# Attention with SyncE in written order: the queries' transposing DMA goes to the head of the next pair, and whole-batch loads are spread differently over two pairs

## The chip, the core and the metric

One core of a Trainium2 chip runs the whole program. Engines are named as in the profile: PE (TensorE), DVE (VectorE), ACT (ScalarE), POOL (GpSimd) and SP (SyncE, which issues nearly all DMAs here). The metric is device time in microseconds (us) of one execution.

## The reference

Three stages follow each other: block-causal attention, a soft mixture of experts, and a feed-forward layer with a squared ReLU. Inputs and outputs are float32; the change touches the first stage alone.

```
q, k, v: (8, 8, 576, 64)
scores = q @ k.T / sqrt(64)
scores = where(block_i >= block_j, scores, -1e9)
scores = scores - max(scores, -1)
attn = exp(scores)
x = attn / (sum(attn, -1) + 1e-9) @ v
x = x.transpose(0, 2, 1, 3).reshape(4608, 512)
x = soft_moe(x, phi, w1, w2)
out = square(relu(x @ w_in)) @ w_out
```

Blocks are 64 positions long, so a row sees whole blocks up to its own.

## The kernel before

Attention works on two heads at a time: 32 pairs, four for each of the 8 batches. In the code `n` is the pair, `bn` its batch and `jn` its place in the batch (0 to 3). `pair(n)` (L997) writes out the steps of one pair in eight slots, and several pairs are under way at once: in `pair(n)` stand the score matmuls of pair n (`scores`, L546), the products with V of pair n-1 (`pv`, L610), the row maxima of pair n+2 (`maxpass`, L468) and the splitting of pair n+3 into fp16 parts (`split`, L419).

A score is the sum of two fp16 matmuls. The first uses the high parts, `t1` and `s1`. The second uses `t2` and `s2`: `t2` holds the low part of the queries and two columns with the negated row maximum, `s2` the keys with constant rows. Both of these come by DMA. The rows are written into `qb` (three buffers), and one DMA transposes `qb` into `t2` (two buffers, by the parity of the pair). `s2copy(n)` (L956) copies the upper half of `s1` into `s2` (two buffers). The keys' own transposing DMA into `s1` stands in `prep_k` (L451) and is issued in slot 0 of the pair three ahead of its own.

The last step of a maximum is `fin` (L521), in slot 6: DVE reduces the partial maxima, writes two columns of `qb` (L531, L534), and the transposing DMA into `t2` follows at once, at L539. It waits for L534 and, since `t2` is reused, for the second matmuls of the pair two before.

Before any of that, `scale` (L373) takes the sums of squares of q and k: ACT squares (L379, written to `junk`), one PE matmul (`ps_ssq`, L386) and eight small DVE steps (L391 to L408) give the factors that `split` needs. In a pair with odd n this is done for two pairs, four and five ahead.

PE and SP run in the order in which the program writes their instructions; DVE, ACT and POOL are ordered by the scheduler. SP's order is set by `pair(n)`: `s2copy(n + 1)` first, then the eight slots. Loads wait as functions in the list `dq`, and `loads(k)` takes the next k of them: three in slot 0 before the slot's steps, one after each of slots 1 to 5, two after slots 6 and 7. Into `dq` go the V loads of pair n+2 (`load_v`, two, or four in the first pair of a batch), the loads of the batch after next (`load_batch`, L351: for k and for q two tails and four main parts of 256 KB each), all of k in the second pair of a batch and all of q in the third, and from pair 7 on a part of the expert weights.

Beside this, DVE and ACT decode the feed-forward layer's `w_in` in tiles (`decode`, L179, five steps, spread one by one over the slots by `dec_step`, L990). After a tile's last step `dec_step` issues the raw load of the tile two later (`load_next`, L943) on SP at once.

```
for i in range(8):
    if i == 0:
        loads(3)
    for f in slot.get(i, []):
        f()
    if i:
        loads(2 if i > 5 else 1)
```

Of the kernel before, what the change touches and what calls it, by code (L numbers as in the profile page):

```python
# [10 lines left out]
F16 = mybir.dt.float16  # L11
# [12 lines left out]
def tile_attn_soft_moe_ffn(  # L24
# [12 lines left out]
    nc = tc.nc  # L37
    B, H, S, D = q.shape
# [8 lines left out]
    NBLK = 2 * NU + 1  # L47
# [192 lines left out]
    def attention():  # L240
# [12 lines left out]
        odd = st_c.enter_context(tc.tile_pool(name="odd", bufs=1))  # L253
        mid = st_m.enter_context(tc.tile_pool(name="mid", bufs=1))
# [10 lines left out]
        NBQ = 3  # L265
        qb = [(even, mid, nat_p)[i].tile([128, NBLK, 128], F16, name=f"qb{i}") for i in range(NBQ)]
# [150 lines left out]
        T = {}  # L417

        def split(n):  # L419
# [45 lines left out]

            return [high_q, lambda: [turn_q(0, 8), turn_q(8, NBLK)], prep_k, low_q]

        def maxpass(n):  # L468
            t1, s1 = T[n][0], T[n][1]
            pmt = pm[n % 2]  # L470
            pf = pmt.rearrange("p a b -> p (a b)")
            ptl = sm_p.tile([128, 5], F32, tag="ptl", name="ptl")
            box = {}

            def part(ps, hp, u, c0):
                nc.tensor.matmul(  # L476
                    ps[:, c0:c0 + 128 * (u + 1)].rearrange("p (s c) -> p s c", c=128), t1[:, 2 * u + hp, :],
                    s1[:, hp:2 * u + 2:2, :], start=(c0 == 0), stop=False,
                )

            def mask(ps, c0, step, cnt):
                o = ps[:, 0:512].rearrange("p (a x) -> p a x", x=128)
                o = o[:, c0 // 128:c0 // 128 + (cnt - 1) * (step // 128) + 1:max(step // 128, 1), 64:128]
                nc.tensor.matmul(o, mrow_l, mrow_r[:, 0:1].to_broadcast([128, 64 * cnt]), start=False, stop=True)  # L484

            def red(ps, o, w, cnt=None):
                i = ps[:, 0:w].rearrange("p (a x) -> p a x", x=min(128, w))
                if cnt:
                    i = ps[:, 0:w].rearrange("p (c a x) -> p c a x", c=cnt, x=128)
                nc.vector.tensor_reduce(out=o, in_=i, axis=AX.X, op=ALU.max)  # L490

            def chunk(i):
                ps = ps_r.tile([128, 512], F32, tag="r", name="ps_max")
                box[i] = ps
                if i < 2:
                    part(ps, i, 0, 0)
                    part(ps, i, 2, 128)
                    mask(ps, 0, 384, 2)
                    red(ps, pf[:, 8 * i + 3:8 * i + 7], 512)
                elif i == 2:  # L500
                    part(ps, 0, 1, 0)
                    part(ps, 1, 1, 256)
                    mask(ps, 128, 256, 2)
                    red(ps, pmt[:, 4:6, 0:2], 512, 2)
                elif i < 5:
                    part(ps, i - 3, 3, 0)
                    mask(ps, 384, 128, 1)
                    red(ps, pmt[:, 3 + i, :], 512)
                else:
                    for hp in range(2):  # L510
                        h0 = 64 * hp
                        nc.tensor.matmul(
                            ps[h0:h0 + 64, 0:512].rearrange("p (s c) -> p s c", c=128) if i == 5
                            else ps[h0:h0 + 64, 0:64],
                            t1[:, 8, h0:h0 + 64],
                            s1[:, hp:8:2, :] if i == 5 else s1[:, 8, h0:h0 + 64],
                            start=True, stop=True,
                        )
                    red(ps, ptl[:, 0:4] if i == 5 else ptl[:, 4:5], 512 if i == 5 else 64)

            def fin():  # L521
                mx = box[4][:, 0:NBLK]
                mv = mx[:, 0:8].rearrange("p (u h) -> p h u", h=2)
                pv4 = pmt.rearrange("p (a b) c -> p a b c", b=2)
                nc.vector.tensor_reduce(out=mv[:, :, 0:3:2], in_=pv4[:, 0:2], axis=AX.X, op=ALU.max)
                nc.vector.tensor_reduce(
                    out=mv[:, :, 1:4:2].rearrange("p h u -> p u h"), in_=pv4[:, 2:4], axis=AX.X, op=ALU.max
                )
                nc.vector.tensor_reduce(out=mx[:, 8:9], in_=ptl, axis=AX.X, op=ALU.max)
                t = qb[n % NBQ]  # L530
                nc.vector.tensor_scalar(  # L531
                    out=t[:, :, 64:65], in0=mx.unsqueeze(2), scalar1=-1.0 / SHIFT, scalar2=None, op0=ALU.mult
                )
                nc.vector.scalar_tensor_tensor(  # L534
                    out=t[:, :, 65:66], in0=mx.unsqueeze(2), scalar=-1.0 / SHIFT, in1=t[:, :, 64:65],
                    op0=ALU.mult, op1=ALU.subtract,
                )
                t2 = (mid, odd)[n % 2].tile([128, NBLK, 128], F16, tag="t2", name="t2")
                nc.sync.dma_start_transpose(out=t2, in_=t.rearrange("p s c -> p (s c)"))  # L539
                T[n][2] = t2  # L540

            return [lambda i=i: chunk(i) for i in range(5)] + [fin, lambda: [chunk(5), chunk(6)]]

        P = {}
# [380 lines left out]
        def wchunks(k):  # L925
            i = nxt[0]
            nxt[0] += k
            return [f for x in range(i, i + k) for f in wchunk((0, 1, 4, 5, 2, 3)[x] if x < 6 else x)]
# [21 lines left out]
        dq = load_pair(0, dict(q=nc.scalar)) + load_pair(1, dict(q=nc.scalar)) + load_pair(2) + load_pair(3)  # L950

        def loads(k):
            for _ in range(min(k, len(dq))):
                dq.pop(0)()
# [31 lines left out]
        work, aux, decq, nraw = [], [], [], [0, 0]  # L986
# [3 lines left out]
        def dec_step():  # L990
            if isinstance(decq[0], int):
                decq[0:1] = decode_in(decq[0])
            decq.pop(0)()
            if decq and getattr(decq[0], "__name__", "") == "load_next":
                decq.pop(0)()

        def pair(n):  # L997
            nonlocal dq, work, aux, decq, ew, early, late_, last, half
            bn, jn = divmod(n, NJ)
# [3 lines left out]
            if jn == 1:  # L1003
                if bn >= 1:
                    work += batch(bn - 1)
                if bn + 1 == B:
                    while decq:
                        dec_step()
                    assert nraw[0] == NRAW, nraw
                    st_in.close()  # L1010
                    wpools["a"] = w_st.enter_context(tc.tile_pool(name="wa", bufs=2, side="right"))
                dq += wchunks({B - 2: 1, B - 1: 2}.get(bn, 0))

            elif jn == 2:
                if n == N - 2:
                    st_a.close()
                    wpools["e"] = w_st.enter_context(tc.tile_pool(name="we", bufs=1, side="right"))
                dq += wchunks({B - 2: 1, B - 1: 2}.get(bn, 0))
            elif jn == 3:
                if bn + 1 == B:  # L1020
                    early, late_, last = batch(bn)
                    work += early
                    st_b.close()
                    st_m.close()
                    wpools["m"] = w_st.enter_context(tc.tile_pool(name="wm", bufs=1, side="right"))
                    wpools["o"] = w_st.enter_context(tc.tile_pool(name="wo", bufs=2, side="right"))
                    dq += wchunks(3)
            elif n == N:
                work += late_
                st_c.close()  # L1030
                wpools["n"] = w_st.enter_context(tc.tile_pool(name="wn", bufs=1, side="right"))
                dq += wchunks(1)
            if n + 2 < N:
                dq += load_v(n + 2)
            if jn in (1, 2) and bn + 2 < B:
                dq += load_batch(bn + 2)[jn - 1]
            if n == 6:
                ew = wchunks(2)
                dq += [lambda i=i: load_in(i) for i in range(2)]
# [34 lines left out]
                at_(4, get(sp, 3))  # L1074
            if n + 1 < N:
                s2copy(n + 1)
            for i in range(8):
                if i == 0:
                    loads(3)
                for f in slot.get(i, []):  # L1080
                    f()
                if i:
                    loads(2 if i > 5 else 1)
                f = aux.pop(0) if aux else None
                if f:
                    f()
                elif decq and i % 8:
                    dec_step()
                for _ in range((i in (1, 3, 4, 6, 7)) if n < N - 3 else 1 if n < N - 1 else 2):
                    if work:  # L1090
                        work.pop(0)()
# [599 lines left out]
```

## Time and profile before

| | |
|---|---|
| Median of 3 runs | 907.48 us (905.68 to 908.2) |
| The profiled execution | 903.58 us |
| Its span, first to last instruction | 901.7 us |
| Attention (span start to the last product with V) | about 0 to 435 us |
| PE busy | 833.1 us (92%) |
| DVE, ACT busy | 673.2 us (75%), 633.4 us (70%) |
| Mean granted TensorE clock | 0.975 of full |

Busy time is the time in which an engine had an instruction at work; idle time before an instruction is put down to what released it. The granted clock is the share of TensorE's full clock that the chip allowed in a stretch. Times in the rows are counted from the start of the span. A pair is cut here at the first `xm` matmul (L628), which belongs to the pair before; the stretch that begins with it is named by the pair whose slots fill it, so the first stretch in the rows below, from 41.21, is pair 1; the others are pairs 3, 4, 7, 8, 10, 11, 15, 19, 23, 24, 26 and 27.

### The profile page before, as it was taken

What the parts mean: (1) busy time and instruction counts of PE and PEld (TensorE: products, weight loads), DVE (VectorE), ACT (ScalarE), POOL (GpSimd) and SP (SyncE); (2) the same over time, 40 slices, a digit from 0 to 9 for tenths busy, and PEclk for the clock granted to TensorE, in tenths of its full rate; (3) what the DMA queues carried; (4) which work ended last, traced back from release to release, by engine and by line L of the source; (5) the groups of instructions that cost most, each with busy time, mean ns of one, the idle gap of its engine ahead of it and who ended that gap; (6) DMA issues with size and microseconds to landing.
All of it is one profiled execution on the core that took longest, in us unless ns stands there. A gap on an engine that the chain in (4) does not pass through costs nothing.

```text
span 901.7 us, 21791 instructions
## 1 busy us (share of the span) xinstructions
PE 833.1 (92%) x8788; PEld 612.3 (68%) x8788; DVE 673.2 (75%) x1600; ACT 633.4 (70%) x1012; POOL 251.2 (28%) x394
## 2 busy tenths in 40 slices
PE   2788989899898998999997799999999999999998
PEld 1455757656565765766733344698998899889897
DVE  5766778878889886765551799888887888888881
ACT  5577767867776787764312689987878888888870
POOL 0243746748484674656200000000000000000000
PEclk9889999999999999999999799999999999999999
DMA  8879797979979586969999700100001000000002
GB/s 161 155 150 172 131 187 143 202 163 205 195 143 201 117 168 106 173 98 271 373 382 380 305 0 1 48 24 25 24 25 40 33 25 24 25 25 24 25 24 48
DMA packets 220357, 113.16 MB, mean 125 GB/s; under 512 B 192096, under 2 KB 194144, under 8 KB 220256
## 3 DMA queue, kind: packets, MB, share of 16 engines
q1 hardware_dynamic: 217600, 111.11, 53.0%
q8 instruction: 69, 1.13, 0.5%
q10 hardware_dynamic: 2656, 0.66, 0.4%
q14 instruction: 32, 0.26, 0.1%
HBM read 78.71 MB, written 9.44 MB: 98 GB/s over the span
## 4 chain that ended last, share of the span: by engine, by line
PE 70%; DMA 10%; POOL 7%; ACT 5%; SPq 2%; DVE 2%; issue 2%; ACTq 0%; POOLq 0%
PE ps_y L1505 14%; PE ps_x L1505 9%; PE ps_z L1505 9%; PE xm L628 6%; PE ps_sc L555 5%; POOL ss L598 5%; PE po L1527 4%; PE ps_hb L1469 3%; DMA s<-s 3%; PE ps_u L729 2%; POOL ul L738 2%; DMA ar_lo<-in_q_dram 2%; PE ps_h L1196 2%; PE ps_x L833 2%; PE ps_max L476 2%
## 5 line engine op out<-in xcount | busy, mean ns | idle before, releaser
L1505 PEld LDWEIGHTS <-ah 128*128 128x128 f16 x1792 | 170.6, 98 | 21.8 <-issue 0.2
L593 ACT ACTIVATE p<-ps_sc,es 128x512 f32<-128x512 f32 x192 | 130.2, 690 | 53.3 <-PE ps_sc L555 25.8
L1438 DVE TENSOR_TENSOR al<-a,ah 128x1024 f16<-128x1024 f32 (+1 forms) x128 | 138.6, 1125 | 17.0 <-ACT ah L1492 15.5
L490 DVE TENSOR_REDUCE pm<-ps_max 128x4 f32<-128x512 f32 x160 | 107.3, 684 | 45.8 <-PE ps_max L484 44.8
L598 POOL TENSOR_TENSOR ss<-p 128x384 f32<-128x384 f32 (+1 forms) x128 | 87.8, 704 | 176.2 <-ACT p L593 175.9
L1492 ACT CAST ah<-a 128x1024 f16<-128x1024 f32 (+1 forms) x128 | 114.4, 936 | 15.2 <-DVE a L1438 13.9
L555 PE MATMUL ps_sc<-t,s 128*128 128x512 f16 (+3 forms) x512 | 109.0, 307 | 9.7 <-DMA s<-s 6.1
L1598 POOL TENSOR_TENSOR ot<-u,p 128x256 f32<-128x256 f32 x16 | 12.5, 781 | 375.1 <-DVE u L1569 359.2
L598 POOL TENSOR_TENSOR ss<-ss,p 128x320 f32<-128x320 f32 (+1 forms) x128 | 104.4, 816 | 16.4 <-ACT p L593 8.6
L1505 PE MATMUL ps_y<-bh,ah 128*128 128x256 f16 x384 | 104.8, 273 | 0.0
L1505 PE MATMUL ps_y<-bl,ah 128*128 128x256 f16 x384 | 104.7, 273 | 0.0
L1505 PE MATMUL ps_y<-bh,al 128*128 128x256 f16 x384 | 104.7, 273 | 0.0
L1360 ACT ACTIVATE r<-ps_hb,alpha 128x1024 f32<-128x1024 f32 x64 | 71.2, 1112 | 33.9 <-PE ps_hb L1469 33.3
L1505 PEld LDWEIGHTS <-al 128*128 128x128 f16 x896 | 87.7, 98 | 10.0
L628 PE MATMUL xm<-p,ar_hi 128*64 128x256 f32 (+3 forms) x512 | 89.9, 450 | 0.0
L1438 DVE TENSOR_TENSOR a<-a 128x256 f32<-128x256 f32 x192 | 76.2, 424 | 3.9
L1505 PE MATMUL ps_x<-bh,ah 128*128 128x256 f16 x256 | 70.1, 274 | 0.0
L1505 PE MATMUL ps_z<-bh,ah 128*128 128x256 f16 x256 | 69.9, 273 | 0.0
L1505 PE MATMUL ps_x<-bh,al 128*128 128x256 f16 x256 | 69.8, 273 | 0.0
L1505 PE MATMUL ps_z<-bh,al 128*128 128x256 f16 x256 | 69.8, 273 | 0.0
L1505 PE MATMUL ps_x<-bl,ah 128*128 128x256 f16 x256 | 69.8, 273 | 0.0
L1505 PE MATMUL ps_z<-bl,ah 128*128 128x256 f16 x256 | 69.8, 273 | 0.0
(255 smaller groups left out, 1832.3 us busy)
## 6 DMA issues: line engine op xcount, KB each, us to landing
wch<-in_moe_w_dram SPq DMA_DIRECT2D x18, 1024.0 KB, 13.1
ar_hi<-in_v_dram SPq DMA_DIRECT2D x64, 128.0 KB, 4.0
raw<-in_moe_w_in_dram SPq DMA_DIRECT2D x16, 512.0 KB, 5.4
out_dram<-ot SPq DMA_DIRECT2D x32, 256.0 KB, 2.2
ar_hi<-in_moe_w_dram SPq DMA_DIRECT2D x6, 1024.0 KB, 8.5
s<-s SPq DMA_DIRECT2D x32, 144.0 KB, 4.0
ar_hi<-in_k_dram SPq DMA_DIRECT2D x16, 256.0 KB, 4.9
ar_hi<-in_q_dram SPq DMA_DIRECT2D x16, 256.0 KB, 4.0
```

The lines of the kernel that those rows point to most:

```text
L476: nc.tensor.matmul(ps[:, c0:c0 + 128 * (u + 1)].rearrange("p (s c) -> p s c", c=128), t1[:, 2 * u + hp, :], s1[:, hp:2 * u + 2:2, :], star ...
L490: nc.vector.tensor_reduce(out=o, in_=i, axis=AX.X, op=ALU.max)
L555: nc.tensor.matmul(ps[:, c0:c0 + w].rearrange("p (s c) -> p s c", c=128), kk[:, 2 * t + hp, :], qq[:, 2 * u0 + hp:8:2, :], start=(c0 == 0 ...
L593: exps[:] = [nc.scalar.activation(out=pt, in_=ps, func=AF.Exp, scale=es[:, 0:1])]
L598: add = lambda o, x, y: nc.gpsimd.tensor_tensor(out=o, in0=x, in1=y, op=ALU.add)
L628: nc.tensor.matmul(box["xm"][64 * hp:64 * hp + 64, 128 * t:512], vs[:, t, hp, :], r, start=(t == 0), stop=(t == 3),)
L1360: nc.scalar.activation(out=r[:, c0:c1], in_=ps[:, c0:c1], func=AF.Relu, **kw)
L1438: sub = lambda o, a, b: nc.vector.tensor_tensor(out=o, in0=a, in1=b, op=ALU.subtract)
L1469: nc.tensor.matmul(ps[:, 512 * j + 256 * a:512 * j + 256 * a + 256], ws[:, 128 * f:128 * f + 128], ctt[:, c0:c0 + 256], start=True, stop=True,
L1492: nc.scalar.copy(v(hl[n % 2][0][:, 2 * kq:2 * kq + 2], s), v(a7[n, kq], s))
L1505: nc.tensor.matmul(acc[:, 0:HM], a[:, k], b[:, k], start=bool(first and k + j == 0), stop=(k == KH - 1 and j == 2), skip_group_check=not f ...
L1527: nc.tensor.matmul(pos[t], g[:, 512 * a + 128 * t:512 * a + 128 * t + 128], tt[:, c, a], start=(c == 0 and a == 0), stop=(c == KH - 1 and ...
```

## The change

It does three things. The transposing DMA of `fin` becomes a function, `turn_qb(n)`. For pairs 0 and 1 it is called where it stood; for the others it is called at the head of the pair before their own, right behind `s2copy`. The loads are taken two before each slot, 16 in a pair instead of 12; the batch loads go into `dq` ahead of V's, and the second pair of a batch takes all of k and the two tails of q, the third pair the four main parts of q. And `dec_step` issues a raw load together with the step after the tile's last one.

```diff
+        def turn_qb(n):
+            t2 = (mid, odd)[n % 2].tile([128, NBLK, 128], F16, tag="t2", name="t2")
+            nc.sync.dma_start_transpose(out=t2, in_=qb[n % NBQ].rearrange("p s c -> p (s c)"))
+            T[n][2] = t2
+
         def maxpass(n):
...
-                t2 = (mid, odd)[n % 2].tile([128, NBLK, 128], F16, tag="t2", name="t2")
-                nc.sync.dma_start_transpose(out=t2, in_=t.rearrange("p s c -> p (s c)"))
-                T[n][2] = t2
+                if n < 2:
+                    turn_qb(n)
...
-            decq.pop(0)()
-            if decq and getattr(decq[0], "__name__", "") == "load_next":
-                decq.pop(0)()
+            f = decq.pop(0)
+            f()
+            if f.__name__ == "load_next" and decq:
+                dec_step()
...
+            if jn in (1, 2) and bn + 2 < B:
+                lk, lq = load_batch(bn + 2)
+                dq += lk + lq[:2] if jn == 1 else lq[2:]
             if n + 2 < N:
                 dq += load_v(n + 2)
-            if jn in (1, 2) and bn + 2 < B:
-                dq += load_batch(bn + 2)[jn - 1]
...
             if n + 1 < N:
                 s2copy(n + 1)
+                if n:
+                    turn_qb(n + 1)
             for i in range(8):
-                if i == 0:
-                    loads(3)
+                loads(2)
                 for f in slot.get(i, []):
                     f()
-                if i:
-                    loads(2 if i > 5 else 1)
```

PE's instructions stand in the same order as before. SP's order changes in every pair. These are SP's instructions of the kernel before around pair 10, from the keys' transposing DMA in its slot 0 to the copy at the head of pair 11 (`ka` and `qb` are the rows to be transposed, `ar_lo` the batch's q and k, `ar_hi` V and weights, `raw` the tiles to be decoded):

```order
L451 DMA_TRANSPOSE s_2661<-ka 128x9x128
L309 DMA ar_hi<-in_v_dram 128x4x64
L361 DMA ar_lo<-in_q_dram 64x4x64
L935 DMA raw<-in_moe_w_in_dram 128x1024
L361 DMA ar_lo<-in_q_dram 64x4x64
L355 DMA ar_lo<-in_q_dram 128x8x64 x2
L539 DMA_TRANSPOSE t_2874<-qb_138 128x9x128
L355 DMA ar_lo<-in_q_dram 128x8x64 x2
L169 DMA ar_hi<-in_moe_w_dram 128x512
L935 DMA raw<-in_moe_w_in_dram 128x1024
L956 DMA s_0_141<-s_2395 64x1152
L309 DMA ar_hi<-in_v_dram 128x4x64 x2
```

The changed kernel, from the copy at the head of pair 10 to the two DMAs at the head of pair 11:

```order
L960 DMA s_1_142<-s_2185 64x1152
L470 DMA_TRANSPOSE t_2663<-qb_140 128x9x128
L355 DMA ar_lo<-in_q_dram 128x8x64 x2
L451 DMA_TRANSPOSE s_2661<-ka 128x9x128
L355 DMA ar_lo<-in_q_dram 128x8x64 x2
L309 DMA ar_hi<-in_v_dram 128x4x64
L314 DMA ar_hi<-in_v_dram 64x4x64 x2
L309 DMA ar_hi<-in_v_dram 128x4x64
L939 DMA raw<-in_moe_w_in_dram 128x1024
L169 DMA ar_hi<-in_moe_w_dram 128x512
L960 DMA s_0_141<-s_2391 64x1152
L470 DMA_TRANSPOSE t_2901<-qb_138 128x9x128
```

The queries' transposing DMA for pair 12 (`t_2874` before, `t_2901` now) stood between two halves of the query loads and ahead of a weight load, a raw load and the copy `s_0_141`; now it stands behind all of them.

DVE's order, which the scheduler makes, changes at the ends of the fourth pairs. Before, in pair 11, from the last partial maximum on (`tin`, `dec_sq` and `raw` belong to the decode, `ps_ssq`, `sig`, `inv` and `es` to `scale`, `ps_max` and `qb` to `fin`):

```order
L490 TENSOR_REDUCE pm_144<-ps_max 128x4
L188 SCALAR_TENSOR_TENSOR tin<-dec_sq,raw 128x512
L525 TENSOR_REDUCE ps_max<-pm_144 128x2x2
L194 TENSOR_SCALAR dec_sq<-tin 128x512
L526 TENSOR_REDUCE ps_max<-pm_144 128x2x2
L200 SCALAR_TENSOR_TENSOR dec_sq<-tin,dec_sq 128x512
L529 TENSOR_REDUCE ps_max<-ptl 128x1
L206 SCALAR_TENSOR_TENSOR tin<-raw,dec_sq 128x512
L531 TENSOR_SCALAR qb_139<-ps_max 128x9
L534 SCALAR_TENSOR_TENSOR qb_139<-ps_max,qb_139 128x9
L391 TENSOR_SCALAR ps_ssq<-ps_ssq 128x4
L392 TENSOR_SCALAR ps_ssq<-ps_ssq 128x4
```

The changed kernel, from the same partial maximum on:

```order
L495 TENSOR_REDUCE pm_144<-ps_max 128x4
L391 TENSOR_SCALAR ps_ssq<-ps_ssq 128x4
L530 TENSOR_REDUCE ps_max<-pm_144 128x2x2
L392 TENSOR_SCALAR ps_ssq<-ps_ssq 128x4
L531 TENSOR_REDUCE ps_max<-pm_144 128x2x2
L396 TENSOR_SCALAR ps_ssq<-ps_ssq 128x4
L534 TENSOR_REDUCE ps_max<-ptl 128x1
L400 TENSOR_SCALAR sig<-ps_ssq 128x4
L536 TENSOR_SCALAR qb_139<-ps_max 128x9
L401 TENSOR_SCALAR inv<-ps_ssq 128x4
L539 SCALAR_TENSOR_TENSOR qb_139<-ps_max,qb_139 128x9
L188 SCALAR_TENSOR_TENSOR tin<-dec_sq,raw 128x512
```

The steps of `scale` stood behind all four of the decode's and behind `fin`; now they alternate with `fin`'s and only one step of the decode stands before the factor `sig` is finished.

## Rows read from the trace of the kernel before

**Rows 1.** The page, part 2: what the DMA engines moved, in 40 equal slices.

```profile
GB/s 161 155 150 172 131 187 143 202 163 205 195 143 201 117 168 106 173 98 271 373 382 380 305 0 1 48 24 25 24 25 40 33 25 24 25 25 24 25 24 48
```

**Rows 2.** Stretches: length, busy PE, PEld, DVE, ACT, POOL (instructions), PEclk, DMA share, GB/s.

```profile
41.21:57.27 16.06, 12.72 (x146) 7.95 (x145) 8.43 (x26) 10.26 (x23) 7.53 (x12) 0.79 0.70 135
...
69.89:82.34 12.45, 10.98 (x143) 6.86 (x143) 6.76 (x21) 9.38 (x21) 4.91 (x8) 0.88 1.06 200
82.34:91.50 9.16, 9.16 (x141) 6.16 (x140) 6.37 (x19) 7.94 (x15) 3.21 (x5) 1.00 0.72 115
116.24:131.57 15.33, 12.76 (x171) 8.07 (x170) 11.26 (x41) 11.75 (x26) 6.80 (x10) 0.98 0.94 206
131.57:142.38 10.81, 10.81 (x150) 6.71 (x149) 7.23 (x17) 7.88 (x15) 2.96 (x5) 0.88 1.01 188
156.57:168.98 12.41, 11.02 (x154) 7.59 (x153) 10.25 (x33) 9.07 (x16) 11.14 (x17) 1.00 1.18 190
168.98:185.91 16.93, 14.00 (x172) 8.55 (x171) 16.20 (x49) 11.51 (x26) 7.62 (x11) 0.90 1.16 233
222.03:238.15 16.12, 12.55 (x172) 8.06 (x171) 15.40 (x48) 11.50 (x26) 7.64 (x11) 1.00 1.19 212
274.26:291.57 17.31, 13.95 (x172) 8.50 (x171) 16.47 (x49) 11.50 (x26) 7.64 (x11) 0.90 1.10 206
327.68:342.94 15.26, 12.37 (x172) 8.07 (x171) 12.85 (x44) 11.07 (x25) 7.22 (x11) 1.00 0.82 164
342.94:352.45 9.51, 9.51 (x149) 6.32 (x149) 6.30 (x14) 7.46 (x14) 2.97 (x5) 1.00 0.56 77
366.31:377.05 10.74, 10.74 (x155) 7.63 (x154) 8.47 (x27) 8.43 (x15) 7.63 (x16) 1.00 0.89 187
377.05:389.72 12.67, 12.25 (x171) 8.07 (x170) 9.44 (x35) 9.72 (x21) 7.51 (x10) 1.00 0.67 99
```

**Rows 3.** PE's waits to 440 us (total, times, longest), then two of them in the timeline.

```profile
PE ps_ssq L386 <- ACT junk L379: 31.1, 12, 10.9
PE ps_sc L555 <- DMA s<-s: 6.1, 3, 2.4
...
49.97 0.59 PE L386 MATMUL ps_ssq<-ssq,ones 128*128 128x2 f32 x2 [2.99 <-ACT junk L379]
...
69.36 0.61 PE L555 MATMUL ps_sc<-t,s 128*128 128x512 f16 x1 [2.21 <-DMA s<-s]
```

**Rows 4.** ACT in the timeline (idle before it, and what ended it).

```profile
181.16 0.68 ACT L379 ACTIVATE junk<-ar_lo 128x576 fp8e4<-128x576 f32 x1 [1.40 <-DMA ar_lo<-in_q_dram]
```

**Rows 5.** SP in the timeline of pair 11: when a DMA was issued, and how long that took.

```profile
173.11 3.16 SPq L539 DMA_TRANSPOSE t<-qb  x1
176.32 1.26 SPq L355 DMA_DIRECT2D ar_lo<-in_q_dram  x2
...
178.78 0.53 SPq L956 DMA_DIRECT2D s<-s  x1
...
181.52 3.77 SPq L451 DMA_TRANSPOSE s<-ka  x1
```

**Rows 6.** SP's waits to 480 us: waiting line, what it waited for, total, times, longest.

```profile
SPq L539 <- DVE qb L534: 81.7, 16, 10.8
```

**Rows 7.** SP in the timeline of pair 1.

```profile
42.69 1.31 SPq L539 DMA_TRANSPOSE t<-qb  x1
44.05 0.58 SPq L355 DMA_DIRECT2D ar_hi<-in_q_dram  x1
```

**Rows 8.** ACT in the timeline of pair 1.

```profile
49.14 0.68 ACT L379 ACTIVATE junk<-ar_hi 128x576 fp8e4<-128x576 f32 x1 [1.63 <-DMA phi<-in_moe_phi_dram]
```

**Rows 9.** From issue to landing: L539 (transposing into t2), then L956 (s2copy).

```profile
DMA to landing us min/median/max: 3.2/4.1/6.9
...
DMA to landing us min/median/max: 2.5/4.0/7.4
```

**Rows 10.** DVE in the timeline of pair 9: the last step of the maximum.

```profile
147.67 0.18 DVE L534 SCALAR_TENSOR_TENSOR qb<-ps_max,qb 128x9 f16<-128x9 f32 x1
```

## Prediction, made before the changed kernel ran

> **What bounds the kernel now.** Read first the table of stretches, cut so that each row is one pair (two heads) of the attention stage, from the first product with V of one pair to that of the next [rows 2]. The columns to look at are the length, PE's busy time and the granted clock. A row in which PE is busy for its whole length is bound by TensorE; a row in which it is not has a hole, and the list of PE's waits says what the hole is [rows 3]. Pairs come in fours (one batch), and the shapes of a four repeat. The row of 342.94 (a first pair of a four) has no hole: 9.51 us, all PE. The row of 377.05 (a fourth pair) takes 12.67 us with 12.25 us of PE. The fourth pairs before it, with the same matmuls, take 15.33, 16.93, 16.12, 17.31 and 15.26 us. These rows hold the time that can be had.
>
> The waits by cause: PE waited 31.1 us for the scalar engine's squares (`junk`, 10.9 us of it before the first matmul) and 6.1 us for the copy `s<-s` into `s2` [rows 3]. Followed back, the first is a load that comes late: the square at 181.16 waited for `ar_lo<-in_q` [rows 4], the queries of the batch after next, whose last two loads left SP at 176.32. Directly before them SP issued the queries' transposing DMA at 173.11, taking 3.16 us, and behind them the copy `s<-s` left at 178.78 [rows 5]. So one instruction holds up both: the transposing DMA at L539, for which SP stood 81.7 us in 16 waits for the vector engine's last step of a maximum (L534), up to 10.8 us at a time [rows 6]. SP works in written order here, and everything behind that wait stands too.
>
> **The change, part by part.** (1) The transposing DMA leaves the end of its pair and goes to the head of the next, behind `s2copy`. It is issued as often as before (32 times), so nothing is saved in issue time; what changes is what stands behind its wait. Behind it were two or four loads and the next `s2copy`; now `s2copy` is ahead of it, and the loads of the pair that has just ended are ahead too. (2) The whole-batch loads are spread 8 and 4 instead of 6 and 6 over the second and third pair of a four and go ahead of V's; the last queries leave in the first two slots of the third pair. Pair 10 begins at 156.57 [rows 2]; behind its head come the transposing DMA, two loads, the keys' transposing DMA and two loads. At the longest issues shown (3.16 us and 3.77 us, loads 0.63 us each [rows 5]) that is 9.5 us, so the last two leave near 167 to 170 where they left at 176.32, and land before the fourth pair's squares ask for them, at about 177. (3) The raw loads of the decode move one step on; they cost nothing, as long as a tile is decoded long after it was loaded (two buffers). (4) PE's order is the same. The vector engine's changes in one place: in the fourth pair the eight small steps on `ps_ssq` now stand ahead of most of the decode instead of behind it, which takes the decode out of their way there.
>
> **The sum.** Fourth pairs (7, 11, 15, 19, 23) against 12.67 us: 2.66 + 4.26 + 3.45 + 4.64 + 2.59 = 17.6 us. The row of 377.05 has no decode in it. What the decode may add is bounded by two third pairs, 12.41 us with it and 10.74 us without [rows 2]: nothing to 1.67 us each; I take the middle, 0.8, five times: 13.6 us are left. Pair 8 ran at a mean clock of 0.88 behind a wait of pair 7 and takes 10.81 us against 9.51: 1.3 us more. The clock goes down to its lower level (1.2 of 2.4 GHz) after such holes, in pairs 1, 3, 8, 11 and 19 of these rows, so what it costs there is in the lengths already.
>
> Pairs 1 to 3: in pair 1 PE waited 2.99 us for a square [rows 3]; the load behind it left at 44.05, just after a transposing DMA that had waited until 42.69 [rows 7]. The new order puts it some 2.5 us earlier; the scalar engine sat idle for 1.63 us before the square at 49.14 [rows 8] (its row names a load of `phi` that landed together with the queries, which is what the square reads), so about that much of the hole goes, and with it perhaps the lower clock, which is PE's 12.72 us against 9.16 of pair 4, 3.56 us. Bounds 0 and 5.8 us (the scalar engine alone needs 10.26 of 16.06); I take 3.5. Pair 2's hole of 2.21 us for `s<-s` goes whole (bounds 0 and 2.21). Pair 3: 12.45 us, of which the scalar engine needs 9.38; bounds 0 and 3.1, I take 2.5. Together 8.2 us.
>
> What is late next: in pair 11 SP issued from 173.11 to 185.29 nearly without a break, eight rows of 11.8 us together [rows 5]. In the new order the transposing DMA for pair 12 stands behind four V loads, a raw load, a weight load and `s2copy`, and leaves at about 174.7 instead of 173.11. Landing takes 4.1 us at the median and 6.9 at most, `s2copy` 4.0 and 7.4 [rows 9]. Pair 12 will want both at about 181.6 (168.98 and 12.67), so the margin is between 3 us and nothing; I take off 0.5 us in each of four batches, 2 us.
>
> Sum: 13.6 + 1.3 + 8.2 - 2.0 = 21 us. The profiled execution took 903.58 us (span 901.7), and 21 off that is 882.5. The median of the runs is 907.48, 3.9 us more; the forecast is told against that: **886 us**. The stages behind attention should only move: weight loads there start when attention's buffers come free.
>
> A rule speaks against this. SP's rows in pair 11 are nearly solid [rows 5], while over a pair such as 8 or 9 SP stands waiting up to 10.8 us [rows 6]. The Trainium skill (Perfetto Trace Analysis, What "DMA-bound" means) counts a kernel as DMA-bound when the issuing engine's sequencer track is solid DMA slices, and says that larger descriptors are what help then. By it, a new order of the same issues would give nothing in the fourth pairs. The rows agree for a stretch of 12 us and not for a whole four.
>
> **The rivals.** A, SP's issue binds: it is so full between the third and fourth pair that the late piece is only another one, the copy or the transposing DMA for the next first pair. For it: the solid rows. Against: SP's long waits elsewhere. Then the fourth pairs stay as they are, and with them pair 8, and only pairs 1 to 3 gain: 907.5 - 8.2 = 899 us. B, slower: the transposing DMA, now ordered late, lands after its pair has begun. The maximum for pair 10 is done at 147.85 [rows 10], pair 10 begins at 156.57: 8.7 us, into which issue and landing must fit. At 1.3 + 4.1 us they do. At the longest shown, 3.77 us of issue and 6.9 of landing, they need 10.6 and PE waits about 2 us; from 8.7 on it decides. If that held in half of the 30 pairs, it would cost some 30 us against a gain of 21 to 23: about 915 us. For it: `s2copy` and up to 12 loads stand ahead of it now. Against: it waits for the same step as before, and the earliest pairs have the same distance. C, hidden anyway: the expert stage moves 370 to 380 GB/s [rows 1] and if its loads, not attention's end, set its pace from the start, it gives the gain back: 905 to 908 us. Against: these loads wait for buffers that attention frees.
>
> **How the numbers follow.** Forecast 0.69, A 0.15, B 0.10, C 0.06. About 0.3% (2.7 us) is what a measurement of this kernel tells from no change. The forecast's own range is its bounds: all at the low side (fourth pairs with the full 1.67 us of decode, half of the early pairs) 14 us, all at the high side 29: 878 to 894. The range given reaches up over A: 877 to 900; B and C are left out. Faster 0.85 (the forecast, A and a little of the others), same 0.06, slower 0.09.
>
> **What would show it.** In the new profile the waits of PE for `junk` should fall from 31.1 us to below 16, those for `s<-s` to below 1; fourth pairs should be 12.7 to 14 us long, pair 8 9.5; SP's long waits should stand at the head of a pair with only two loads and the keys' transposing DMA behind. The prediction is wrong if PE waits for `t<-qb` at first pairs (B), if the fourth pairs keep 15 to 17 us (A), or if attention ends 20 us earlier and the kernel does not (C).

## Result, and the profile after

| | before | changed |
|---|---|---|
| Median, four runs each on the same chip | 907.71 us (905.68 to 908.2) | 876.52 us (874.0 to 878.1) |
| Profiled execution (span) | 903.58 us (901.7) | 875.46 us (873.7) |
| First product with V (start of pair 1) | 41.21 us | 40.41 us |
| Last cut (start of the last pair's product with V) | 434.88 us | 410.83 us |
| From there to the end | 466.8 us | 462.9 us |

The ratio is 0.9658 with the interval 0.9628 to 0.9688: 31.2 us faster by the medians, 28.0 us by the two profiled spans. The forecast was 886.0 us in 877 to 900. It lies 9.5 us too high, and the result 0.5 us below the range. A second comparison on another chip gave 877.86 against 907.49 us, 0.9683 (0.9649 to 0.9716).

The same table of stretches of the changed kernel answers to [rows 2] (length, busy PE, PEld, DVE, ACT, POOL, PEclk, DMA share, GB/s):

```profile
40.41:53.89 13.48, 10.20 (x146) 6.62 (x145) 9.07 (x38) 10.04 (x23) 7.66 (x12) 1.00 0.95 178
53.89:67.79 13.90, 11.03 (x143) 7.21 (x142) 6.28 (x21) 9.27 (x20) 3.91 (x6) 0.88 1.14 199
67.79:77.41 9.62, 9.57 (x144) 6.40 (x143) 7.06 (x22) 9.49 (x22) 6.10 (x9) 1.00 0.98 191
...
111.31:123.63 12.32, 12.32 (x171) 8.09 (x170) 10.17 (x32) 10.63 (x25) 6.30 (x9) 1.00 1.21 211
123.63:133.15 9.52, 9.52 (x150) 6.32 (x149) 8.62 (x26) 8.55 (x16) 4.26 (x7) 1.00 1.17 217
...
159.82:172.67 12.85, 12.62 (x171) 8.15 (x171) 12.44 (x41) 11.29 (x26) 6.86 (x11) 1.00 1.04 209
...
208.85:221.69 12.84, 12.61 (x171) 8.15 (x170) 12.44 (x41) 11.27 (x26) 6.84 (x11) 1.00 1.15 198
...
257.88:270.39 12.51, 12.38 (x171) 8.09 (x170) 12.27 (x39) 11.49 (x26) 6.85 (x11) 1.00 1.15 203
...
306.59:319.11 12.52, 12.39 (x172) 8.09 (x171) 12.05 (x43) 10.74 (x25) 6.87 (x11) 1.00 0.94 163
```

Pairs 1, 2, 3 come first, then 7, 8, 11, 15, 19 and 23. Compare length with PE's busy time: in all five fourth pairs PE is now idle for at most 0.23 us, and after pair 3 no stretch of a pair shows a clock below 1.00. The gain by place, before minus after: the start 0.80; pairs 1 to 3 2.58 - 1.28 + 2.83 = 4.13; the fourth pairs 3.01 + 4.08 + 3.28 + 4.80 + 2.74 = 17.91; pair 8 1.29; all other pairs -0.08. That is the 24.05 us by which attention's last cut moved. The stretch behind it gave 3.95.

PE's waits to 415 us answer to [rows 3] (total, times, longest):

```profile
PE ps_ssq L386 <- ACT junk L379: 17.6, 5, 10.7
...
PE ps_sc L559 <- DMA t<-qb: 3.0, 1, 3.0
PE ps_max L481 <- DMA s<-ka: 2.9, 1, 2.9
```

The squares fell from 31.1 us to 17.6, and what is left of them lies in pair 1 and ahead of it: no square is waited for after 53 us. `s<-s` is gone. One wait is new: `s<-ka`, the keys' transposing DMA, at 61.56 us, which is why pair 2 became longer in this execution; in the second profile of the changed kernel it was 0.63 us, and pair 2 took 11.89 us.

SP around the head of pairs 10 and 11, in the timeline, answers to [rows 5], and the scalar engine's square to [rows 4]:

```profile
151.15 0.52 SPq L960 DMA_DIRECT2D s<-s  x1
151.77 2.56 SPq L470 DMA_TRANSPOSE t<-qb  x1
154.38 1.97 SPq L355 DMA_DIRECT2D ar_lo<-in_q_dram  x2
156.45 2.31 SPq L451 DMA_TRANSPOSE s<-ka  x1
158.81 1.22 SPq L355 DMA_DIRECT2D ar_lo<-in_q_dram  x2
...
165.24 0.52 SPq L960 DMA_DIRECT2D s<-s  x1
165.86 1.57 SPq L470 DMA_TRANSPOSE t<-qb  x1
```

```profile
168.70 0.69 ACT L379 ACTIVATE junk<-ar_lo 128x576 fp8e4<-128x576 f32 x1
```

The last query loads left SP at 158.81 instead of 176.32, and the square ran at 168.70 without waiting, 12.5 us earlier than at 181.16. Pair 11 itself begins 9.2 us earlier here (159.82 against 168.98); counted from its start, the loads left 8.4 us and the square ran 3.3 us earlier. The copy and the next transposing DMA stand directly behind each other.

SP's own waits to 405 us answer to [rows 6]:

```profile
SPq L470 <- DVE pm L495: 31.4, 7, 6.1
SPq L960 <- PE ps_sc L559: 24.6, 12, 5.9
SPq L470 <- DVE qb L539: 11.3, 4, 3.6
```

SP still stands at the transposing DMA and at the copy, but from 62 to 415 us no wait of PE is put down to a DMA.

### The profile page after: what moved, and what is told of

Read it like the earlier page. It is cut to its first block, busy times and chain, and to the rows that moved or that the text cites. A ratio compares the mean times of both kernels' runs of the same rounds, so it can differ in the third digit from the quotient of the medians.

```text
span 873.7 us, 21803 instructions
## 1 busy us (share of the span) xinstructions
PE 820.3 (94%) x8788; PEld 609.2 (70%) x8788; DVE 668.1 (76%) x1600; ACT 631.6 (72%) x1012; POOL 252.3 (29%) x394
## 4 chain that ended last, share of the span: by engine, by line
PE 69%; ACT 9%; POOL 8%; DMA 5%; DVE 4%; issue 3%; SPq 1%; ACTq 0%; DVEq 0%; POOLq 0%
PE ps_y L1510 14%; PE ps_x L1510 10%; PE ps_z L1510 10%; PE xm L632 5%; POOL ss L602 5%; PE ps_sc L559 5%; PE po L1532 4%; PE ps_hb L1474 3%; DMA wch<-in_moe_w_dram 3%; ACT p L597 2%; POOL ul L742 2%; PE ps_u L733 2%; PE ps_max L481 2%; PE ps_x L837 2%; PE ps_h L1201 1%
## 5 line engine op out<-in xcount | busy, mean ns | idle before, releaser
L1497 ACT CAST ah<-a 128x1024 f16<-128x1024 f32 (+1 forms) x128 | 114.4, 936 | 14.9 <-DVE a L1443 13.6
L1603 POOL TENSOR_TENSOR ot<-u,p 128x256 f32<-128x256 f32 x16 | 12.5, 782 | 374.5 <-DVE u L1574 358.6
L559 PE MATMUL ps_sc<-t,s 128*128 128x512 f16 (+3 forms) x512 | 106.6, 303 | 3.2 <-DMA t<-qb 3.0
L632 PE MATMUL xm<-p,ar_hi 128*64 128x256 f32 (+3 forms) x512 | 87.2, 440 | 0.0
L481 PE MATMUL ps_max<-s,t 128*128 128x128 f16 (+3 forms) x256 | 62.1, 308 | 9.3 <-DVE pm L495 5.4
```

The lines of the kernel that those rows point to most:

```text
L481: nc.tensor.matmul(ps[:, c0:c0 + 128 * (u + 1)].rearrange("p (s c) -> p s c", c=128), t1[:, 2 * u + hp, :], s1[:, hp:2 * u + 2:2, :], star ...
L559: nc.tensor.matmul(ps[:, c0:c0 + w].rearrange("p (s c) -> p s c", c=128), kk[:, 2 * t + hp, :], qq[:, 2 * u0 + hp:8:2, :], start=(c0 == 0 ...
L632: nc.tensor.matmul(box["xm"][64 * hp:64 * hp + 64, 128 * t:512], vs[:, t, hp, :], r, start=(t == 0), stop=(t == 3),)
L1497: nc.scalar.copy(v(hl[n % 2][0][:, 2 * kq:2 * kq + 2], s), v(a7[n, kq], s))
```

## The experiments

Four theories are set against each other. **1**: SP works in written order, and what stands behind a late wait leaves late. **2**: the vector engine's order, which the scheduler makes anew, gave the fourth pairs their time. **3**: the gain behind attention is TensorE's granted clock in that execution, not the change. **4**, formed after the first four runs: with the transposing DMA moved, SP next stands at the decode's raw load.

Ratios are against the kernel before, run beside each on the same chip. The cut and the rest are those of the table above, in the profiled execution.

| Kernel | median, us | ratio (interval) | last cut | rest |
|---|---|---|---|---|
| before | 907.71 | 1 | 434.88 | 466.8 |
| transposing DMA alone | 890.38 | 0.9790 (0.9754 to 0.9826) | 423.83 | 466.2 |
| loads alone | 886.83 | 0.9738 (0.9710 to 0.9765) | 422.23 | 466.3 |
| raw load alone | 907.47 | 1.0012 (0.9984 to 1.0039) | 439.23 | 462.8 |
| transposing DMA and raw load | 886.38 | 0.9784 (0.9750 to 0.9818) | 418.59 | 465.1 |
| transposing DMA and loads | 884.71 | 0.9717 (0.9683 to 0.9752) | 416.19 | 466.3 |
| all three (the change) | 876.52 | 0.9658 (0.9628 to 0.9688) | 410.83 | 462.9 |
| the change again | 877.86 | 0.9683 (0.9649 to 0.9716) | 410.04 | 463.0 |
| transposing DMA in slot 4 | 951.98 | 1.0465 (1.0438 to 1.0493) | 485.51 | 464.5 |
| loads 6 and 6 | 876.12 | 0.9655 (0.9623 to 0.9687) | 410.86 | 463.7 |
| pair 1: keys earlier | 879.98 | 0.9693 (0.9666 to 0.9720) | 411.85 | 466.7 |
| pairs 1 and 2 in new order | 876.36 | 0.9670 (0.9641 to 0.9698) | 408.42 | 465.8 |
| and earlier queries | 875.65 | 0.9676 (0.9644 to 0.9709) | 410.15 | 462.6 |
| fillers in the expert stage | 877.28 | 0.9669 (0.9641 to 0.9697) | 410.54 | 466.7 |

The lengths of the fourth pairs 7, 11, 15, 19 and 23, and of pairs 1 to 3 together, by the same cut:

| Kernel | 7 | 11 | 15 | 19 | 23 | 1 to 3 |
|---|---|---|---|---|---|---|
| before | 15.33 | 16.93 | 16.12 | 17.31 | 15.26 | 41.13 |
| transposing DMA alone | 12.32 | 16.14 | 16.54 | 13.79 | 13.71 | 37.60 |
| loads alone | 13.33 | 15.92 | 16.16 | 14.25 | 12.88 | 38.56 |
| transposing DMA and raw load | 12.31 | 15.59 | 13.78 | 13.78 | 13.45 | 37.41 |
| transposing DMA and loads | 12.31 | 13.47 | 15.07 | 13.96 | 12.89 | 36.76 |
| all three | 12.32 | 12.85 | 12.84 | 12.51 | 12.52 | 37.00 |

### The transposing DMA alone

```diff
             if n + 1 < N:
                 s2copy(n + 1)
+                if n:
+                    turn_qb(n + 1)
```

> The kernel before, with the queries' transposing DMA alone moved to the head of the next pair; the loads keep their 6/6 spread, their rates and their places behind V's. Theory 1 (SP's written order: what stands behind the wait of the transposing DMA leaves late): the copy s<-s no longer stands behind that wait, so PE's waits for s<-s fall from 6.1 us to under 1 and pair 2 loses its hole of 2.21 us; the last query loads of the fourth pairs leave some 3 us earlier, so the squares' waits fall by a part only, about 2 to 3 us in each of five fourth pairs. 12 to 17 of the 28 us between the two profiled executions. Theory 2 (the vector engine's order, made anew by the scheduler, gives the fourth pairs their time): the same 4 us for pairs 1 to 3, and the fourth pairs gain only where the scale steps stand ahead of the decode's.

PE's waits for `s<-s` went, the squares' waits stayed:

```profile
PE ps_ssq L386 <- ACT junk L379: 27.4, 11, 10.7
PE ps_sc L559 <- DMA t<-qb: 6.7, 4, 3.1
```

SP's waits to 405 us, and SP in the timeline:

```profile
SPq L939 <- DVE tin L206: 36.8, 4, 10.8
```

```profile
163.07 6.28 SPq L355 DMA_DIRECT2D ar_lo<-in_q_dram  x4
```

The last four query loads left from 163.07 to 169.35, and pairs 11, 15, 19 and 23 wait 1.3 to 1.6 us each for the squares. The waits are those that theory 1 names, and the gain is 11.8 us by the profiled executions and 19 by the ratio, around its 12 to 17. Its 2 to 3 us in each fourth pair did not come: pairs 7 and 19 gained 3.0 and 3.5, pairs 11 and 23 0.8 and 1.6, and pair 15 lost 0.4, for there a new wait of 2.60 us for `t<-qb` followed that for the squares. The wait of SP was not expected: it stood up to 10.8 us at the raw load, until the decode's last step (L206) had read the buffer. Before, the raw load's longest wait was below 1 us. One wait at the front of SP's queue had been replaced by another.

### The loads alone

```diff
-            if jn in (1, 2) and bn + 2 < B:
-                dq += load_batch(bn + 2)[jn - 1]
...
+                loads(2)
```

(With `load_batch` ahead of `load_v`, as in the change.)

> The kernel before, with the loads alone changed (8 and 4, two in every slot, ahead of V's); the transposing DMA stays at the end of its pair. Theory 1: the query loads leave before that wait, so the squares' holes of the fourth pairs go whole (about 17 us) and only s<-s stays (6 us of PE's waits, since the copy still stands behind the transposing DMA). Theory 2: the fourth pairs gain according to the vector engine's order alone. If the move of the transposing DMA is what counts (the change's first part), this gains under 5 us.

```profile
PE ps_ssq L386 <- ACT junk L379: 17.9, 5, 10.7
PE ps_sc L555 <- DMA s<-s: 8.0, 4, 3.1
```

The waits are as theory 1 says: after pair 1 no square is late, and `s<-s` now costs 8.0 us, since the copy still stands behind the transposing DMA. In pair 11 the copy left SP at 170.69, and the scores waited for it until 177.15. So pairs 11 and 15 kept 15.92 and 16.16 us, and the fourth pairs gained 8.4 us, half of the 17 expected: this wait took the place of the other.

### Both of these, without the later raw load

```diff
-            f = decq.pop(0)
-            f()
-            if f.__name__ == "load_next" and decq:
-                dec_step()
+            decq.pop(0)()
+            if decq and getattr(decq[0], "__name__", "") == "load_next":
+                decq.pop(0)()
```

(Against the changed kernel.)

> The changed kernel with the decode's raw loads taken at once after their step, as before. Theory 1: no difference beyond 2 us: the raw load is one transfer behind the query loads. Theory 2: if the raw load or the vector engine's order (both of which this moves back in part) gave the fourth pairs their time, 5 to 15 us of the gain go.

PE's waits, SP's waits to 405 us, and SP in the timeline:

```profile
PE ps_sc L559 <- DMA t<-qb: 7.1, 5, 3.0
```

```profile
SPq L939 <- DVE tin L206: 34.3, 5, 10.0
```

```profile
180.73 7.26 SPq L939 DMA_DIRECT2D raw<-in_moe_w_in_dram  x2
188.10 0.85 SPq L960 DMA_DIRECT2D s<-s  x1
189.05 2.22 SPq L470 DMA_TRANSPOSE t<-qb  x1
```

Now neither squares nor `s<-s` are late, and `t<-qb` is: four waits behind the prologue's. Two raw loads took 7.26 us of SP's time, the transposing DMA left at 189.05 instead of 187.70 in the changed kernel, whose pairs 12 to 15 begin within 0.05 us of these, and the next two left 3.0 and 2.1 us later than there. The last of them, at 216.29, landed 7.2 us after its issue, and PE waited 2.04 us for it at 223.57, in pair 15. The last cut is 5.4 us later than in the change. The two parts do not add: alone they moved it by 11.05 and 12.65 us, together by 18.7 (by the ratios 19 and 24 us, and 26). Theory 1 had said 2 us at most; the raw load's wait is what it left out.

### The raw load's part

The same lines of `dec_step`, put into the kernel before alone, and together with the transposing DMA.

> The kernel before, with the decode's raw load alone one step later. Theory 4: before, SP was held at the transposing DMA for so long that it never waited for the raw buffer (no wait over 0.6 us there), so nothing is gained: within 3 us of before. Rival (the vector engine's order around the raw load is what counts): 4 to 9 us gained.

> The kernel before with two parts of the change: the queries' transposing DMA at the head of the next pair, and the decode's raw load one step later; the loads as before (6/6, behind V's). Theory 4 (with the transposing DMA moved, SP next stood at the raw load, up to 10.8 us, until the decode had read the buffer; the later raw load takes that wait away): SP's waits at the raw load fall from 36.8 us to under 2, and 4 to 10 us are gained against the transposing DMA alone (890 us): 880 to 886. Rival (the raw load's place matters only together with the new loads, or it is the vector engine's order): within 3 us of 890.

Alone it does nothing (1.0012), as expected. With the transposing DMA, SP's wait for L206 at the raw load is gone (SP's waits, then SP in the timeline):

```profile
SPq L939 <- DVE x L847: 0.5, 1, 0.5
```

```profile
214.39 5.08 SPq L355 DMA_DIRECT2D ar_hi<-in_q_dram  x4
```

The `t<-qb` wait of 2.60 us in pair 15 went with it. But the squares of the fourth pairs still wait 1.1 to 1.7 us, because the query loads are late anyway (second row; this kernel keeps their old place), and the ratio, 0.9784 against 0.9790, shows no gain. Its attention is 5.2 us shorter in the profile, 4.4 of them in pairs 15 and 16, where that wait was, but the ratio decides: such a gain is not shown. So the later raw load pays where the loads are early, 5.4 us of attention, and is not shown to pay elsewhere.

**Theory 2** finds no support: in none of these kernels does PE wait for a step of `scale` on the vector engine. And fourth pairs have the same length with different orders. In pair 19 the first decode step (L188) ran ahead of the first step of `scale` (L391) in the kernel "loads 6 and 6" below, and behind eight steps of `scale` and `fin` in the change; the pair took 12.52 and 12.51 us (first two rows: 6 and 6; then the change):

```profile
269.17 0.75 DVE L188 SCALAR_TENSOR_TENSOR tin<-dec_sq,raw 128x512 f32<-128x512 f32 x1 [0.54 <-ACT dec_sq L185]
269.92 0.16 DVE L391 TENSOR_SCALAR ps_ssq<-ps_ssq 128x4 f32<-128x4 f32 x1
```

```profile
268.48 0.16 DVE L391 TENSOR_SCALAR ps_ssq<-ps_ssq 128x4 f32<-128x4 f32 x1
269.50 1.13 DVE L188 SCALAR_TENSOR_TENSOR tin<-dec_sq,raw 128x512 f32<-128x512 f32 x1
```

With the order of 6 and 6, the loads alone took 14.25 us in this pair, with a wait of 1.20 us for `s<-s`. In pair 7 the order went the other way, the decode step ahead of `scale` in the change (121.92, then 122.98) and behind its first step before (126.91, then 129.05), and the pair is 3.01 us shorter. An experiment that fixes the vector engine's order in all fourth pairs was not made.

### A dose for rival B

`turn_qb(n + 1)` behind the loads of slot 4 instead of at the head of the pair.

> The changed kernel with the transposing DMA moved on from the head of the pair into its fifth slot, behind ten loads, a dose for rival B of the prediction (too late for the pair that reads it). Theory 1: it leaves some 4 to 6 us later; where the margin at the first pairs is between nothing and 3 us, as the prediction said, PE waits 1 to 5 us for t<-qb in most of 30 pairs: 30 to 100 us slower than the changed kernel. Rival: the margin is larger than was forecast (no wait for t<-qb appeared at a first pair), and it costs under 10 us.

```profile
PE ps_sc L559 <- DMA t<-qb: 64.8, 18, 8.1
```

951.98 us, some 74 above the change: rival B's mechanism is real, with 17 waits of up to 8.1 us behind the prologue's one. The DMA left 14 us behind the copy there (151.82 and 166.07), in the change 0.6; the dose was larger than the 4 to 6 us expected. The margin of the change is small all the same. The DMA for pair 12 left at 165.86; its time to landing, and the matmul that first reads it, without a wait:

```profile
DMA to landing us min/median/max: 6.0/6.0/6.0
...
172.15 0.59 PE L559 MATMUL ps_sc<-t,s 128*128 128x512 f16 x2
```

That leaves some 0.3 us, and in pair 8 some 0.2 (8.3 us to landing). The second profile of the changed kernel has one such wait of 1.11 us, in pair 3.

### How the loads are spread

All keys in the second pair and all queries in the third, as before, still two in a slot and ahead of V's.

> The changed kernel with the whole-batch loads spread 6 and 6 as before (all keys in the second pair of a four, all queries in the third), still ahead of V's and two in each slot. Theory 1 (what counts is that no query load stands behind a late wait): the queries' two small loads move one pair later, the last query loads leave about 1.3 us later: less than 3 us slower than the changed kernel, no new wait over 1 us in the fourth pairs. Rival: the 8/4 spread is what makes it; 5 to 15 us of the gain go.

No difference (876.12 us; fourth pairs 12.52 to 12.53). The new spread is not what counts; what is left of the loads' part is the rate and the place ahead of V's, and these two were not separated.

### The early pairs

```diff
-                loads(2)
+                loads((1, 1, 0, 0, 2, 2, 2, 2)[i] if n == 1 else 2)
```

> The changed kernel, where pair 1 alone issues two batch loads ahead of the keys' transposing DMA and the other six behind it (before: all eight ahead). Theory (the new wait of 2.9 us for s<-ka in pair 2, with the half clock behind it, is the place in the queue): the transposing DMA leaves some 4 us earlier, the wait goes, pair 2 falls from 13.9 us to 10 to 10.7, and the kernel takes 3 to 5 us less than the changed one. Rival (the vector engine's late ka sets it, or the loads that now stand behind come late): no gain, or the squares of pair 3 wait.

Pair 2 fell to 10.89 us, nearly as expected, pair 3 rose to 11.78: the next transposing DMA left only at 72.27 and PE waited 1.99 us for it. The rival had the outcome, by another mechanism than it named. So the next kernel holds V's loads back in pair 2 as well (`else 2 * (i < 2) if n == 2 else 2`):

> The changed kernel, where in pair 1 only two batch loads stand ahead of the keys' transposing DMA, and in pair 2 V's four loads go behind the next queries' transposing DMA instead of ahead of it (in the variant with pair 1 alone it left at 72.27 us, 5 us after its values were ready, and pair 3 waited 2 us for t<-qb). Theory (the hole of pairs 1 to 3 moves along SP's queue, from s<-ka to t<-qb): both waits go; pairs 1 to 4 together 43.5 to 45 us against 45.4 to 48.1 in the runs so far; the kernel 1 to 3 us faster than the changed one. Rival (the early pairs are bound by their late squares at 47 and 52 us, whatever the queue's order): 45 us or more, no gain.

Its stretches for pairs 1 to 4, and their sum:

```profile
41.29:54.75 13.46, 10.20 (x146) 6.63 (x145) 9.06 (x38) 10.02 (x23) 7.55 (x12) 1.00 0.97 179
54.75:65.43 10.68, 9.79 (x144) 6.42 (x143) 6.40 (x22) 9.91 (x21) 4.59 (x8) 1.00 0.98 194
65.43:75.46 10.03, 9.68 (x143) 6.46 (x143) 6.98 (x19) 8.98 (x21) 4.34 (x7) 1.00 1.34 194
75.46:84.62 9.16, 9.16 (x141) 6.17 (x140) 7.14 (x24) 8.42 (x17) 5.60 (x8) 1.00 0.87 185
41.29:84.62 43.33, 38.82 (x569) 25.68 (x568) 29.59 (x101) 37.34 (x79) 22.08 (x32) 1.00 1.04 187
```

43.33 us, against 46.16 and 45.67 in the two profiles of the change: of the two waits 0.4 and 0.6 us are left, and the clock stays whole. The 1 to 3 us expected of the kernel's time did not show: 0.9670 is not told apart from the change's 0.9658 and 0.9683.

> As the one before, and batch 1 loaded two at a step instead of one in the prologue, so that its queries leave SP ahead of the second transposing DMA. If the late squares (waits of 1.3 to 1.9 and 2.0 us at 47 and 52 us) are late loads, they go, and pair 1 falls from 13.5 us to 10 to 11.5; the kernel 3 to 5 us faster than the changed one. Rival: the loads take the queues from the first transposing DMAs, and the first pair begins later by as much.

Pair 1 fell to 11.83 us, and the hole moved on again: pair 2 waited 3.06 us for `t<-qb`, whose DMA left at 60.70, behind six batch loads that took from 51.86 to 58.79; its values were ready at 52.4. The gain of 3 to 5 us did not come (0.9676).

### Behind attention

> The changed kernel once more, beside the three below on the same chip. If the 3.9 us by which the stretch behind attention was shorter in its first profile (462.9 us against 466.2 to 466.8 in the kernel before and in three variants) belong to the change, they come again. Rival: they are the granted clock of one execution (6.9 us at half clock in the expert stage there, 13.7 to 17.1 us in the others); then this stretch varies with that stretch of half clock, and between 462 and 467 us.

> The changed kernel with five filler matmuls ahead of each of the last six weight groups of the expert stage, where TensorE waits 0.5 to 1 us each for weights; their result is not read. Theory 3 (the length of the stage behind attention varies with the clock that is granted there): the half-clock stretches at the stage's end go, and the stretch behind attention is 461 to 463 us in the profile. Rival: it is the weights' arrival that sets this stretch; then fillers cost up to 3 us and the stretch is 463 to 467 us.

The first 80 us behind the last cut, one row for each kernel: before, the change, the raw load alone, the transposing DMA with the loads, the pairs 1 and 2 in new order, the transposing DMA in slot 4, the fillers (columns as in [rows 2]).

```profile
434.88:514.88 80.00, 68.72 (x603) 30.61 (x602) 39.95 (x137) 25.78 (x57) 4.62 (x8) 0.89 1.02 377
```

```profile
410.83:490.83 80.00, 68.06 (x614) 32.22 (x613) 42.14 (x140) 29.89 (x62) 4.67 (x8) 0.96 0.99 361
```

```profile
439.23:519.23 80.00, 69.50 (x615) 32.89 (x614) 42.40 (x141) 30.05 (x63) 4.65 (x8) 0.94 1.00 369
```

```profile
416.19:496.19 80.00, 68.87 (x605) 31.23 (x603) 39.78 (x136) 26.41 (x58) 4.66 (x8) 0.89 0.99 364
```

```profile
408.42:488.42 80.00, 68.67 (x606) 31.71 (x605) 39.78 (x137) 26.74 (x58) 4.65 (x8) 0.91 0.99 360
```

```profile
485.51:565.51 80.00, 69.00 (x610) 32.01 (x609) 40.44 (x139) 28.09 (x60) 4.66 (x8) 0.91 0.97 353
```

```profile
410.54:490.54 80.00, 69.88 (x635) 32.90 (x633) 39.78 (x137) 25.99 (x57) 4.67 (x8) 0.94 0.99 364
```

The column to read is PEclk. In the thirteen profiles without fillers, those with 0.94 or 0.96 here have a rest of 462.6 to 463.7 us (the change twice, the raw load alone, 6 and 6, earlier queries), those with 0.89 or 0.91 one of 464.5 to 466.8 us. The raw load alone, whose attention ends at 439.23, has the short rest; the transposing DMA with the loads, whose attention ends 18.7 us earlier than before's, has the long one. So the 3.95 us go with the clock of the execution and not with the change: theory 3, by comparing executions. The change's own second profile had the short rest again, which alone would have spoken for the change; two variants that hold all of it (pair 1 with earlier keys, pairs 1 and 2 in new order) had the long one. The one experiment on theory 3 missed its expectation: with fillers the clock was 0.94, as in the executions with a short rest, and yet the rest took 466.7 us instead of 461 to 463, within the 463 to 467 of its rival. Whether the fillers' own time or the weights' arrival took back what the clock gave is not separated. Why the clock fell in one execution and not in another is open.

## Why the prediction was too high

The mechanism was right: one wait of SP's queue held up query loads and the copy, and both went. By the prediction's own marks, PE's waits for squares were to fall below 16 us (17.6, missed), `s<-s` below 1 (0), fourth pairs to 12.7 to 14 us (12.32 to 12.85, three of five below it), pair 8 to 9.5 (9.52). What failed are sizes in the sum: the two amounts taken off for what might go wrong, the decode in the fourth pairs (4.0 us) and new waits (2.0 us), came to nothing, and the early pairs were put at twice what they gave. These errors cancel in part, which is luck. The terms, 21 us against 28.0 between the two profiles:

- **Fourth pairs, 13.6 against 17.9.** "What the decode may add ... I take the middle, 0.8": it adds at most 0.18 us in a pair, and three of the five are shorter than 12.67. Of the third pairs' 1.67 us, from which the bound came, 1.23 are a wait for the partial maximum `pm` (pairs 10, 14, 18 and 22); pairs 6 and 26, without the decode, do not have it, and the fourth pairs do not either.
- **New waits, -2.0 against 0.** The transposing DMA left where it was foreseen: 6.0 us after the start of pair 11 (165.86 and 159.82), forecast 5.7 (174.7 and 168.98). The margin came out at its lower end, some 0.3 us for pair 12, and no wait followed: the first pairs 12, 16, 20 and 24 are all PE. That nothing had to be taken off owes something to luck.
- **Pairs 1 to 3, 8.2 against 4.1** (and 0.8 at the start, not forecast). Pair 1 gave 2.58 (3.5 forecast) and pair 3 2.83 (2.5). Pair 2 was to gain 2.21 and lost 1.28: of the transposing DMAs only the queries' was followed through the new order, not the keys', which in pair 1 now stands behind eight loads. (In the second profile pair 2 gained 0.74.)
- **Pair 8**, 1.3 against 1.29.
- **The raw load, "they cost nothing"**: right as a cost, wrong as a part of no weight. Without it SP's wait moves to the raw buffer and 5.4 us of attention go.
- **Behind attention, 0 against 3.95**: the clock of two executions, as shown above. This is no failure of the mechanism, but it stands in the difference between the profiles.
- **Profile and median.** The 3.9 us between the profile of before and its median were carried over whole. The gain by medians was 31.2 us, 3.2 more than by profiles. The profile of before is a short one: its 903.58 us lie below all four timed executions (905.68 to 908.2), while the profile of the change, 875.46, lies among its own (874.0 to 878.1). The raw load alone, another kernel but equal to it in time, had 398.5 us between the first and the last cut where before had 393.7, with first pairs behind a hole at up to 10.53 us instead of 9.51, at a lower clock. That holes cost more clock in other executions than in the one read is the likely reason, and is not shown beyond this one run.
- **The bounds.** Added up from the terms, the low side comes to 12.7 us and not 14 (8.35 off the fourth pairs, half of the early pairs, the 2 us off), the high side to 28, or 30 without the 2 us, and not 29. Of the two comparisons the first lies 0.5 us below the range and the second (877.86) inside it.

Rival A fell: SP's rows between pairs 10 and 11 are as solid as before [rows 5], from 151.15 to 170 with hardly a gap, and the fourth pairs lost their holes. By the rule of the Trainium skill (Perfetto Trace Analysis, What "DMA-bound" means) such a solid sequencer track is a bound of its own that asks for larger descriptors; here the same issues in another order gave 3.4%, so the measurement decides against reading it that way for a stretch. Rival B did not come, and the dose shows that it would have, had the DMA left later; in pair 15 of the transposing DMA with the loads, 2.1 us later and a longer landing were enough. Rival C fell: attention ended anywhere from 408 to 486 us, and the rest kept its length but for the 4 us that go with the clock.

## What to carry to other kernels

An engine that issues DMAs in written order has one front. Taking a wait away from it moves the front to the next instruction whose operand is not ready (here the copy, then the raw buffer, then the keys), so follow every waiting instruction through the new order, and do not cost a "harmless" reordered load at nothing before its buffer's last reader has been found. Parts of such a change do not add: by their ratios each alone gave 0, 19 or 24 us here, all together about 30.

## What the runs showed that was not expected

- Behind the same wait of 0.94 us at the start of the expert stage, the granted clock fell soon after in some executions and not in others. That one fall does not decide the rest (6 and 6 had it and the short rest, the transposing DMA with the raw load had it not and took 465.1 us); what goes with the rest is the mean clock of the first 80 us, and two profiles of two kernels can differ by 4 us for that alone.
- Loads of the same 256 KB took 0.63 us each to issue in [rows 5] and 1.57 us each (6.28 for four) at 163.07 in the transposing DMA alone. What slows them was not tried.
